# Residual picks and decoder picks turned by transposing transfers inside SBUF, decoder in blocks of four rows, a new order of steps

## The chip, the cores and the metric

The kernel runs on one core of one Trainium2 chip. The metric is the device time of one execution in microseconds (us). The text calls the engines by short names: PE is TensorE (PEld its weight loads), DVE is VectorE, ACT is ScalarE, POOL is GpSimd, SP is SyncE. SP computes nothing here; it issues transfers, in the order in which the program holds them, and SPq is that queue. A name such as L802 is line 802 of the kernel.

## The reference

A small neural codec: a depthwise convolution of three taps, SiLU, four stages of residual vector quantization with codebooks of eight entries, and a second depthwise convolution over the sum of the entries picked.

```python
B, T, D, K = 2, 16000, 512, 3
Nq, C = 4, 8

def reference(x, dw_enc, codebooks, dw_dec):
    xp = pad(x, one row of zeros before and after)
    z = silu(sum(xp[:, i:i+T, :] * dw_enc[i] for i in range(K)))
    res, q = z, 0
    for s in range(Nq):
        cb = codebooks[s]
        d2 = |res|^2 - 2 * res @ cb.T + |cb|^2        # (B, T, C), in bfloat16
        sel = cb[d2.argmin(-1)]
        q, res = q + sel, res - sel
    qp = pad(q, one row of zeros before and after)
    return sum(qp[:, i:i+T, :] * dw_dec[i] for i in range(K))
```

All tensors are bfloat16; 32,000 rows of 512 channels go in and as many come out.

## The kernel before

**Tiles.** The rows of each batch are cut into nine tiles, 18 in all; a tile holds G rows on each of 128 partitions, with G = 16 for fourteen of them and 6 and 8 for the two at each end (SIZES). GH = G/2 is the number of row pairs.

**Stages of a tile.** `load` brings x in, one transposing transfer of 128x512 for each of the G rows plus up to two for the rows at the rim (L567, L575, L581, all issued by SP), so that channels lie on partitions (XT, two buffers). `front` computes the three taps on DVE (TA, TB, L609 and L407) and the exponential on ACT (EX, L614), adds 1 (L616); `front2` takes the reciprocal on ACT (L626) and multiplies (L407): the result is Z in one of four ZB buffers. `select` runs the first three quantizer stages: products with the codebook entries and the squared norm on PE (`gram`, L638 and L645), then a chain of small DVE operations that ends in a one-hot pick (`is_equal`, L407) per stage, with a small PE transpose (L723, evicted as OT at L727 on ACT or L728 on DVE) and correction (L733) in between. `resid` forms the residual after three stages on PE: it adds Z (L796, 64x64 pieces with IDENT, UP and DOWN) and the picked rows (L802, 64x128 pieces: OHR times WR), and evicts it back into ZB (L822 on ACT, L823 on DVE). Then come the fourth stage's products and its pick (L849, L850 and L407), and `back`, the decoder: PE multiplies the picks (OHW) with a table that holds codebook entries times decoder taps (WDEC, L883, with L885 and L887 at a tile's rim), the result is evicted into YB (L892 on ACT, L893 on DVE) and stored by SP (L915; two transfers or more for four rows).

**The two turnings.** The picks come out with rows on partitions and must lie with picks on partitions to be a weight or a moving operand of PE.

- `rows`: after the third pick, OHD (the picks of three stages, each twice, 64 columns a row) is turned by GH PE transposes of 128x128 into one PSUM bank (L755) and copied into OHR by ACT or DVE (L760 where DVE does it).
- `windows`: after the fourth pick, OHA (the picks of all four stages) is turned by four PE transposes for each row pair, each filling 32 partitions (L772), and copied into OHW by ACT or DVE (L778). Each pair's window spans four rows, the pair and one neighbour on either side, so that one product of full height gives one output row: two products of 128x512 a pair, and two more at the tile's rim.

OHA is filled by DVE for stages 1, 2 and 4; POOL copies the third stage's pick from OHD into it (L715), and copies stages 1 and 2 from OHA twice into OHD (L718).

**The order.** Nothing runs in the order in which it is written. Every step is added to a `Plan` with an engine, an estimated cost, what it reads and writes and which PSUM banks it takes (four pairs of banks). `order()` then lays out one fixed sequence for each engine, by the steps' ranks (RANK) and by a model of when each can start; a step that may go to ACT or DVE (`either`: taps, plus1, OT, the copies of both turnings, evictions of resid and back) is placed by a rule of slack (SLACK) or by a list (ON_ACT, ON_DVE). SP's sequence of loads and stores is laid out in the same way. While PE would idle for long, filler products are put in (L935).

Of the kernel before, what the change touches and what calls it, by code (L numbers as in the profile page):

```python
# [16 lines left out]
class Plan:  # L17
# [10 lines left out]
    GATE = {"resid": (1.0, 2.0), "back": (1.0, 2.0), "win0": (0.6, 1.5), "win3": (0.6, 1.5), "score0": (0.25, 1.4), "score3": (0.25, 1.4)}  # L28

    def __init__(self, pairs, slack, window, quota, margin, ranks, fixed):  # L30
        self.steps, self.writer, self.readers = [], {}, {}
        self.pairs, self.slack, self.window, self.quota, self.margin, self.ranks, self.fixed = pairs, slack, window, quota, margin, ranks, fixed
# [38 lines left out]
    def order(self):  # L71
# [4 lines left out]
        assert len(rank) == len(steps)  # L76
        users = [[] for _ in steps]
# [26 lines left out]
        def look(s, e):  # L104
            t = max(at[s["n"]], clock[e])
            if s["take"]:
                if s["dest"] and held[s["dest"]] >= self.quota[s["dest"]]:
                    return inf
                t = place(s["take"][0], t)[0]
                return t + late(s["mm"], t, s["c"])  # L110
            if isinstance(s["e"], tuple) and s["n"] in self.fixed:
                if e != self.fixed[s["n"]]:
                    return inf
            elif isinstance(s["e"], tuple):
                ends = {q: max(at[s["n"]], clock[q]) + s["c"][q] for q in s["e"]}
                least, most = self.slack[s["k"][0]]
                off = ends["ACT"] - ends["DVE"]
                if (e == "ACT" and off > least) or (e == "DVE" and off <= least and off < most):
                    return inf
            if s["mm"]:  # L120
                t += late(s["mm"], t, s["c"])
            return t
# [17 lines left out]
        while len(out) < len(steps):  # L140
# [47 lines left out]
            if s["free"]:  # L188
                if s["free"]["dest"]:
                    held[s["free"]["dest"]] -= 1  # L190
                for j in s["free"]["banks"]:
                    banks[j] = end + self.LATENCY[e] + self.margin[2]
# [12 lines left out]
def kernel(  # L205
# [8 lines left out]
    nc = tc.nc  # L214
# [21 lines left out]
    SLACK = {"setup": (8.44, -17.24), "taps": (-10.16, -13.78), "plus1": (-7.56, 14.47), "decide": (9.58, -18.78), "win0": (-11.29, -2.01), "resid": (15.34, 2.59), "win3": (13.16, -12.88), "back": (17.64, 2.16)}  # L236
    QUOTA = {"ACT": 4, "DVE": 4}
    MARGIN = (0, 0, 0, 1)
    WINDOW = {"PE": 0.14, "ACT": 0.41, "DVE": 0, "POOL": 0.79, "SP": 0.05}
    DIGITS = "0123456789abcdefghijklmnopqrstuvwxyzABCDEFGHIJKLMNOPQRSTUVWXYZ"  # L240
    RANK = ("5W5X711A60616g5N69683w3x3y3z7M7N8keXeY8Y8Z909192939495969798999a9b9R9S9T9U9V9W9X9Y9Za0a1a2a3a4a5a6a7a8eZf0f1f2f3f4f5f6f7"
            "f8f9fafbfcfdfefffgfhfifjhtjikV9cflfmfnfofpfqfrfsftfufv9dfwfzfAfBfCfDfEfFfGfHfIfJfKfLfMfNfOg6g7g8g9gagbgc9egdgegfggghgigj"
            "gkglgmgngogpgqgrgsgtgugvgwgxgygzgAhZi0i1i2i3i4i5i6i7i8i9ianMnNnOnPnQnRnSnTet8CtktltmtntotptqtrknhrjUdJm7kgaLaMaN2r2s2t2v"
            "2w2x2y2z2A2B2D2E2G2H2L2M2O2P2Q2S2T2U2V2W2X2Y2Z323334353637bhbicueocvhQepluhRnzlvjyjzjAm0m1m2m37s7thShTkMkNkOnZo0o16m6d6n"
            "6l6e6k6j6h6f6iiNiOiPiQiRiSiTiUbUeFr8r9rarbrcrdrerfiitscz5Ijf9f7J7K7L3Q3R3X40444c4e4g4h4i4j4k4o4p4z4A4E4G4I4M4N4P4S4T4U4V"
            "4Z5b5g5l5o5y5z8d8ehpkxhqookyrxopsZry5q5hnEiMe41P4qdVdWbYbZdKdLdMgTgUjQjRjS6z6E6u6C6v6A6q6F6p6t6y6w6s6x6r6B6D6o7z7A7B7C7D"
            "7E7F7Gd88LdBdCdDdEdFdGdHdIjJjtks29tZ2k7eal3hdnbJrg1g1B2b4x1m1u1q0X3U1E5p0R1w3Y1peW171Uc0dw1j0O8f1VhW0U1b1avc0Q1ieV2m5rBb"
            "enhahffUejl4hbj8hhnAhLpulOpMhVn0hvlSm90ZqsqeoMsovKvSx1mvmwgBgChChDhEixiykdkekfliljmUmVmWoqorpApBpC6W6H6Z786N6O6Q6P6S6U6X"
            "6M6V6R736J6Y6T1G1J1K1IeQ3G3H2hlN3q211Z20222j3p3M26v5tyoCu1vJfW9q3ghXdb9ktj1o6I0ooR2g1v0a062n0i3s030r2o020u1H2f1O1h07050p"
            "0e0C0S0B0v0s100j0f0l5QtEcogQr3bQbeho8QbNb98vcQhwipl1jZdSpaeKeHeSkWkp8X8px4wWwUj75fidieiliminitiuiGiHiIj5j6jojpjqjKjLjWjX"  # L250
            "jYbXc1c2c3c4c5c6c7cacbcccecfchcickclcmn6nCnUn5qq1rzUwTuxvvhU11k09yBaBuBt3vij3nvCd0tHeg457n5P8I8J8K0J1d241W2c0K0Y1c19io0y"
            "1s2a1e1R2u2i1T1C0x0D0A1z4d180E0L2N3jpL1D8U7Y2C5av2s2sKs3thsLtRtiuktSuYulvruZvGvsvMvH9s8A4Yatcs8j8V7UahvbjOsPmzmAmXmYmZn3"
            "n4n9nanbndneninjnknpnqnsntnubfbgbjbkbobpbqbrbsbtbwbybAbBbCbDbEbF0N3m3k3ltg0V0T3FqNajBzujC1wcyQyBBvCct6kIk7kYpVtVaOaBw4bT"
            "bS9z4r4t53585t525K625H4W5m5YoZ7koY707PrE4s4J517o825w7f5x88878t9h5T9i8i8q7ObOmumqmTngoLpEnooT4CqZoBnWpOpHrCp2seba9B8cdveT"
            "484u311F9Gs6scfPfQhxhyhzj3j4kFkGkHmimjo6o7o8pIpJrkrlrmamanaoaqasauavayaAaCaEaGaIaKaPaRaTaUpSsDrNpZt0s0qbq2zhw5wkwKx5xewV"
            "z0yW9DA03uuV9lwJ5B7rb842dlbW4addarsx7d7h1L153d1l161n3A3L3b3E3a494R4Q5F3c2lcN3074cM2R2F1S3T3S2q25gD67o9oaobocodoeofogohoi"
            "ojokolompconnXk9jTvzr7rSqf4l5i1YeCt7t8qLqMrsrtrurGrHrVrWrXs7s8sgshsisFsGsVsWsXcAcCcDcEcFcGcIcLcOcPcRcScTcVcWcXcYcZ6a5J56"
            "5s7Vt5oXm4vq3Z5u5v8s3t9puf5Svhxq43xp5jyZ13e0e27RmSiftd76757XbLdoe38EdUcp72rOrDrRphrMkwuc7ud24H8nbM5E7c8WnYpwpxwHhd5Aib3N"
            "h0nFdsdydtdNdzdYdOecdZekedereleAeseGeB5G8z3Ib6cw8lvYwgtWrwzgzFqvqwqBqCqDqGqHqPqQqRqUqVr0r1r2r5r6rhrirj9H9I9J9K9L9M9N9O9P"
            "9Qa9aaabadaeafagn7n84b3Wu63VsE86893ewd7H5c4B5ksTte9A7l9EB377oJsdq4eDcxcyuih8h9ic4D59274X643K1k2K4y14bV2d0z3f2p9xoV5D2J3o"  # L260
            "47280M3J1X0P1N3O6b7v3i1f23bR4fmBmCmDmEmFmGmHmImJmKmLmMmNmOmPmQmR9m8x7Td3ef6cvy8B8SakvNvOqgqhrorprqrYrZslsmsnt9tatvtwtxtX"
            "tYumunuoaxazaDaFaHaJaQaSaVaWaYaZb0b1b2b3xUxVb4eyhGebeapR7isNcny0wIlJsud7dgya7jxfyhBgpzzG7WB63PdAe746kAkmyJ7Z7qw6wrhklg55"
            "5Z6L4K7y5O6KmgiknL5R8379lL4L7p7m50lPn1stnydX575V5n4OlxoEuzuAuBuC9CuDuEuFuGuHuIuJuKuLuMuNuO8y9g8acUapbIbGbvrPrBvAjaw7whwl"
            "wmwawpwnwMwBwzwXwRxgx2x9xjxixnxzxvkQkRkTkUkXkZl2l5l7l9lclelhlllnlolrlstItJp1pvC063C23ru24n7w7x841MAJcJ4mADA3qktGq9wQq8fX"
            "fSt1mrmslpsbvws1pT8T8Rbcbu9vai9FwoxmxlwCxxxNA9lEzi9obP7abHn27g8wyRzDAPbKaXcjcqvfu3u7u4uau8udubugueupuhusuquuutuwuvsssfBo"
            "qYwbltnKvgycxLyrynxGxCxExDxFxOxPxWxXxYy5y6yeyfygypyEyxzbyylTlUlWlXlYlZm5m6m8mambmcmdmemhmkmmmnyoyqy38Nq68180qpzloDwx8F85"
# [47 lines left out]
    def sb(shape, dt, name):  # L314
        return const.tile(list(shape), dt, name=name)
# [657 lines left out]
```

## Time and profile before

| | |
|---|---|
| median of 3 runs | 629.38 us (628.88 to 632.24) |
| the profiled execution | 627.0 us, its span from first to last instruction 625.1 us |
| granted TensorE clock, mean | 0.971 |
| ACT busy | 512.7 us, 82% |
| POOL busy | 79.3 us, 13% |
| transfers | 72.05 MB, 283 transposing loads, 131 stores |

How to read the views: the busy lines give microseconds, the share of the span and the number of instructions of each engine. The row of digits cuts the span into 40 equal slices of 15.6 us and gives the busy share in tenths. A group's row gives line, engine, operation, output and input with their shapes, the number of instructions, the total busy time, the mean of one in nanoseconds, and the engine's idle time just ahead of them with what ended it. The chain is followed back from the last instruction to whatever released each step. A wait view gives who waited for whom: total, times, longest.

### The profile page before, as it was taken

The numbers are of one execution on the slowest core, as the hardware profiler recorded it, in microseconds if no ns is written. First come the engines' busy times: TensorE is split into PE (matmuls) and PEld (weight loads), VectorE is DVE, ScalarE is ACT, GpSimd is POOL, SyncE is SP. The second block draws the span as 40 slices with busy tenths as digits, with TensorE's granted clock in tenths as the row PEclk, the third lists the DMA queues.
The fourth block names the chain that finished last, engine by engine and source line by source line (L and its number), as shares of the span: only waits on it lengthen the run. The fifth ranks groups of instructions, "written<-read, shape, count | busy, mean of one in ns | idle before, by whom it ended". The sixth has DMA issues, their size and how long they took to land.

```text
span 625.1 us, 26738 instructions
## 1 busy us (share of the span) xinstructions
PE 517.6 (83%) x12065; PEld 241.8 (39%) x12147; DVE 554.8 (89%) x1126; ACT 512.7 (82%) x398; POOL 79.3 (13%) x92
## 2 busy tenths in 40 slices
PE   4968867797977979788788869778979997989995
PEld 1434323433443443434334433434344344443442
DVE  6898999999989999999899999999989998984532
ACT  4454497759695999999887999998979999979765
POOL 2001000141100211101010202011022220010000
PEclk9999979898999999897799999999999999999999
DMA  5455455464461476766653585757575335042424
GB/s 115 91 98 90 101 95 86 95 176 91 78 93 44 92 184 97 193 95 185 119 142 62 82 138 94 225 96 153 94 190 88 131 62 173 3 153 94 164 98 150
DMA packets 163976, 72.05 MB, mean 115 GB/s; under 512 B 155567, under 2 KB 155599, under 8 KB 163862
## 3 DMA queue, kind: packets, MB, share of 16 engines
q1 hardware_dynamic: 163646, 69.90, 51.4%
q8 instruction: 95, 1.56, 1.1%
q10 hardware_dynamic: 216, 0.43, 0.2%
q14 instruction: 19, 0.16, 0.1%
HBM read 0.43 MB, written 32.77 MB: 53 GB/s over the span
## 4 chain that ended last, share of the span: by engine, by line
DVE 45%; PE 25%; ACT 13%; issue 7%; DMA 5%; SPq 4%; DVEq 0%; ACTq 0%
DVE ZB L407 11%; DVE TB L609 8%; PE ps L802 7%; PE ps L796 6%; PE ps L645 5%; DVE TA L407 5%; DVE TA L609 3%; ACT EX L626 3%; SPq L567 3%; DVE EX L616 3%; ACT EX L614 3%; DMA out_dram<-YB 3%; ACT YB L892 3%; PE ps L883 3%; ACT ZB L822 2%
## 5 line engine op out<-in xcount | busy, mean ns | idle before, releaser
L614 ACT ACTIVATE EX<-ZB 128x4096 bf16<-128x4096 bf16 (+2 forms) x36 | 115.1, 3199 | 35.5 <-DVE ZB L407 33.6
L802 PE MATMUL ps<-OHR,WR 64*128 64x512 bf16 (+1 forms) x1024 | 137.5, 381 | 0.9 <-issue 0.6
L892 ACT CAST YB<-ps 128x1024 bf16<-128x1024 f32 x121 | 115.5, 1027 | 17.3 <-PE ps L883 4.9
L822 ACT CAST ZB<-ps 128x1024 bf16<-128x1024 f32 (+1 forms) x121 | 116.9, 1003 | 15.1 <-PE ps L802 14.9
L626 ACT ACTIVATE EX<-EX 128x4096 bf16<-128x4096 bf16 (+2 forms) x36 | 114.7, 3195 | 0.2
L645 PE MATMUL ps<-ZB 128*32 128x64 bf16 x8064 | 90.5, 198 | 16.4 <-issue 8.8
L718 POOL COPY OHD<-OHA 128x256 bf16<-128x256 bf16 (+2 forms) x36 | 51.2, 1421 | 380.6 <-DVE OHA L407 365.3
L609 DVE TENSOR_SCALAR TB<-XT,WENC 128x2048 bf16<-128x2048 bf16 (+2 forms) x144 | 97.2, 682 | 0.2
L645 PEld LDWEIGHTS <-ZB 128*32 128x32 bf16 x8064 | 76.8, 95 | 52.0 <-issue 46.3
L935 PE MATMUL ps<-MSK,IDENT 128*128 128x512 bf16 x288 | 73.1, 393 | 11.3 <-issue 3.7
L883 PE MATMUL ps<-WDEC,OHW 128*128 128x512 bf16 x213 | 65.0, 386 | 12.1 <-ACT YB L892 3.6
L407 DVE TENSOR_TENSOR ZB<-ZB,EX 128x4096 bf16<-128x4096 bf16 (+2 forms) x36 | 72.7, 2018 | 2.0 <-ACT EX L626 1.8
L802 PEld LDWEIGHTS <-WR 64*128 64x128 bf16 x1024 | 40.1, 95 | 87.5 <-issue 61.0
L407 DVE TENSOR_TENSOR ZB<-TA,TB 128x4096 bf16<-128x4096 bf16 (+2 forms) x36 | 72.8, 2021 | 0.3
L407 DVE TENSOR_TENSOR TA<-TA,TB 128x4096 bf16<-128x4096 bf16 (+2 forms) x36 | 72.6, 2017 | 0.3
L796 PE MATMUL ps<-ZB,IDENT 64*64 64x512 bf16 (+1 forms) x512 | 51.3, 388 | 12.0 <-ACT ZB L822 5.8
L796 PE MATMUL ps<-ZB,DOWN 64*64 64x512 bf16 (+1 forms) x512 | 53.4, 404 | 0.1
L796 PE MATMUL ps<-ZB,UP 64*64 64x512 bf16 (+1 forms) x512 | 50.8, 381 | 0.0
L609 DVE TENSOR_SCALAR TA<-XT,WENC 128x2048 bf16<-128x2048 bf16 (+2 forms) x72 | 48.2, 677 | 0.6 <-DMA XT<-in_x_dram 0.3
L935 PEld LDWEIGHTS <-IDENT 128*128 128x128 bf16 x311 | 29.7, 101 | 43.2 <-issue 14.6
L616 DVE TENSOR_SCALAR EX<-EX 128x4096 bf16<-128x4096 bf16 (+2 forms) x36 | 39.4, 1095 | 3.4 <-ACT EX L614 3.4
L883 PEld LDWEIGHTS <-OHW 128*128 128x128 bf16 x252 | 21.8, 99 | 37.6 <-issue 18.4
(123 smaller groups left out, 487.5 us busy)
## 6 DMA issues: line engine op xcount, KB each, us to landing
out_dram<-YB SPq DMA_DIRECT2D x33, 448.0 KB
out_dram<-YB SPq DMA_DIRECT2D x28, 512.0 KB
XT<-in_x_dram SPq DMA_TRANSPOSE x283
out_dram<-YB SPq DMA_DIRECT2D x30, 60.0 KB
out_dram<-YB SPq DMA_DIRECT2D x31, 2.0 KB
out_dram<-YB SPq DMA_DIRECT2D x2, 224.0 KB
YB<-in_dw_dec_dram ACTq DMA_DIRECT2D x1, 384.0 KB
out_dram<-YB SPq DMA_DIRECT2D x1, 384.0 KB
```

The lines of the kernel that those rows point to most:

```text
L407: add("DVE", cost, key, lambda: nc.vector.tensor_tensor(out=out, in0=a, in1=b, op=op), reads, writes, **kw)
L609: lambda dst=dst, src=src, w=w: nc.vector.tensor_scalar(out=dst, in0=src, scalar1=w, scalar2=None, op0=ALU.mult),
L614: add("ACT", act(2 * R), ("exp", n, h), lambda: nc.scalar.activation(v(ex), Z, ACT.Exp, scale=-1.0), zt, [("EX", sl), "ACTTAB"], hold="E")
L616: lambda: nc.vector.tensor_scalar(out=ex, in0=ex, scalar1=1.0, scalar2=None, op0=ALU.add), [], [("EX", sl)])
L626: nc.scalar.add_instruction(mybir.InstActivation(name=nc.get_next_instruction_name(), engine=mybir.EngineType.Activation, func=ACT.Reciprocal,
L645: nc.tensor.matmul(o[HB * q:HB * (q + 1), u * ZW:(u + 1) * ZW].rearrange("p (s c) -> p s c", s=2), lhsT=blk, rhs=both, start=False, stop=( ...
L796: nc.tensor.matmul(ps(boxes[m])[to, 512 * u:512 * u + nk * P], lhsT=dia[h, h], rhs=Z[h, i, g0 + u:g1:2, :], start=start, stop=False)
L802: nc.tensor.matmul(ps(boxes[m])[:, 512 * u:512 * u + nk * P], lhsT=WR[v][half[u], i * P:(i + 1) * P], rhs=W[half[u], g0 // 2:g1 // 2, :], ...
L822: either({"ACT": act_psum(2 * nk * P), "DVE": dve(2 * nk * P)}, ("resid", n, m / len(units)), lambda: nc.scalar.copy(dst, src()), lambda: ...
L883: nc.tensor.matmul(o, lhsT=W[:, k, PADC:PADC + P], rhs=WDEC[u], start=True, stop=not wrap)
L892: either({"ACT": act_psum(1024), "DVE": dve(1024)}, key, lambda dst=dst, box=box: nc.scalar.copy(dst, ps(box)), lambda dst=dst, box=box: n ...
L935: nc.tensor.matmul(PS[j // 2][:, 512 * (j % 2):512 * (j % 2) + NMK * ZW], lhsT=IDENT, rhs=MSK.rearrange("p u w -> p (u w)"), start=True, s ...
```

## The change

**Turning by transfers.** `rows` issues, for each four row pairs, one transposing transfer on SP from OHD to OHR; `windows` issues one from OHA to OHW. The PE transposes, their PSUM banks and their copies on ACT or DVE are gone. A tile of 16 rows has two of the first and one of the second, each 128x512; 50 in all.

```diff
     def rows(st, key):
         n, GH = st["n"], st["GH"]
         OD, W = OHD[n % 2], OHR[n % 2]
-            for k in range(GH):
-                nc.tensor.transpose(pwb[:, k * P:(k + 1) * P], OD[:, 2 * k:2 * k + 2].rearrange("p g s c -> p (g s c)"), IDENT)
...
-        either({"ACT": act_psum(GH * P), "DVE": dve(GH * P, 1.92)}, key, lambda: nc.scalar.copy(dst, src()), lambda: nc.vector.tensor_copy(dst, src()),
-               [], [("OHR", n % 2)], free=box, after=[j])
+        for k0 in range(0, GH, 4):
+            ks = slice(k0, min(k0 + 4, GH))
+            add("SP", 1.36, key, lambda ks=ks: nc.sync.dma_start_transpose(out=W[:, ks, :],
+                in_=OD[:, 2 * ks.start:2 * ks.stop].rearrange("p g o s c -> p (g o s c)")), [("OHD", n % 2)], [("OHR", n % 2, k0 // 4)], tail=1.5)

     def windows(st, key):
-            for k in range(GH):
-                for s in range(Nq):
-                    nc.tensor.transpose(pwb[NC * s:NC * (s + 1), k * P:(k + 1) * P],
-                                        A[:, s, 2 * k:2 * k + 4, :].rearrange("p g c -> p (g c)"), IDENT)
...
+        A, W, nb = OHA[n % NOH], OHW[n % NW], (st["G"] + 3) // 4
+        add("SP", 1.36, key, lambda: nc.sync.dma_start_transpose(out=W[:, 0:nb, PADC:PADC + P], in_=A[:, 0:4 * nb].rearrange("p g s c -> p (g s c)")),
+            [("OHA", n % NOH)], [("OHW", n % NW)], tail=1.5)
```

**Layouts.** OHA becomes rows by stages by entries, without the two rim rows and their memsets; a block of four rows fills 128 columns. OHW holds GM/4 blocks instead of GM/2 windows, with 16 columns of padding on either side instead of 2. OHD's columns are two copies of four stage slots. Stages 1 and 2 write their picks into small tiles of their own (OH), and POOL's third copy brings all three stages from OHD to OHA at once.

```diff
-    OHA = [sb([P, Nq, GM + 2, C], BF16, f"OHA{b}") for b in range(NOH)]
-    PADC = 2
-    OHW = [sb([P, GHM, P + 2 * PADC], BF16, f"OHW{b}") for b in range(NW)]
+    OHA = [sb([P, GM, Nq, C], BF16, f"OHA{b}") for b in range(NOH)]
+    PADC = 16
+    OHW = [sb([P, GM // 4, P + 2 * PADC], BF16, f"OHW{b}") for b in range(NW)]
...
-    OHD = [sb([P, GM, SL, C], BF16, f"OHD{b}") for b in range(2)]
+    OHD = [sb([P, GM, 2, Nq, C], BF16, f"OHD{b}") for b in range(2)]
...
-    WDEC = [sb([P, D], BF16, f"WDEC{v}") for v in range(4)]
+    WDEC = [sb([P, D], BF16, f"WDEC{v}") for v in range(6)]
...
-                add("POOL", 1.5, key(5), lambda OH=OH: nc.gpsimd.tensor_copy(OH, OHD[b][:, 0:G, 4, :]), [("OHD", b)], [("OHA", n % NOH)])
+                add("POOL", 1.5, key(5), lambda: nc.gpsimd.tensor_copy(A[:, 0:G, 0:3, :], OHD[b][:, 0:G, 0, 0:3, :]), [("OHD", b)], [("OHA", n % NOH)])
```

**Decoder in blocks of four rows.** Windows no longer overlap. An output row has one product of full height with its own block; a row at a block's rim (its first or its last) has one more of half height (64 rows of a neighbouring block). Of a block of four rows, two full products come first, then the other two and the two halves; both pairs' evictions follow the second group. The products of all blocks are chained in order.

```diff
+        def terms(g):
+            m, r, last = g // 4, g % 4, G - 1
+            out = [(None, m, 0, r)]
+            if r == 0:
+                out.append((1, m - 1, 0, 4) if g else (last % 4 // 2, last // 4, -1, 4 if last % 4 == 3 else 5))
+            if r == 3 or g == last:
+                out.append((0, m + 1, 0, 4) if g < last else (0, 0, 1, 4))
+            return out
...
+            whole = [q for q in todo if q[3][0] is None]
+            first = whole[:2] if len(ks) > 1 else []
+            rest = whole[len(first):] + [q for q in todo if q[3][0] is not None]
+
+            def mms(group, boxes=boxes):
+                for g, i, n1, (h, blk, shift, v) in group:
+                    at = slice(None) if h is None else slice(HF * h, HF * h + HF)
+                    nc.tensor.matmul(ps(boxes[g // 2])[:, 512 * (g % 2):512 * (g % 2) + 512], lhsT=W[at, blk, PADC + shift:PADC + shift + P],
+                                     rhs=WDEC[v][at], start=i == 0, stop=i == n1)
+            j = bchain[0]
+            for k, group in zip(ks, (first, rest) if first else (rest,)):
+                j = add("PE", ...)
+            bchain[0] = j
```

**Score of the fourth stage.** Its eviction was one DVE step of two operations (L849 and L850). The second, the copy of the products into PR3, becomes a step of its own that ACT or DVE may do.

**The order.** RANK is a new string. SLACK, ON_ACT and ON_DVE are replaced by WHERE, a string with one letter for each step that may go to ACT or DVE. The windows within which the planner lets a better rank go first change a little. A PSUM bank is free once all its evictions are done.

```diff
-    WINDOW = {"PE": 0.14, "ACT": 0.41, "DVE": 0, "POOL": 0.79, "SP": 0.05}
+    WINDOW = {"PE": 0.1, "ACT": 0.43, "DVE": 0, "POOL": 0.52, "SP": 0.09}
...
-    ON_ACT = (434, 554, 564, ...)
-    ON_DVE = (374, 393, 407, ...)
+    WHERE = ("DDDDDDDDDDDDDDDDDDDDAAAAAAAADDDDDDDDDDDDDDDADADAADAAAADDDDDDDDDDDDDDDDAAAAAAAADAAAAAAAAADDDDDDDDDDDDDDDAAAAAAAAADAAAAAAAA"
...
```

234 lines of the change are left out of this document (105 added, 129 removed), and 5 rows, old and new, of the table ON_DVE.

## The prediction

> **What bounds the kernel now.** I read the busy lines first, then the table by stage, then the waits of the transfer queue SP, then the chain that ended last, and last the rows of the edited lines.
>
> ```profile
> span 625.1 us, 26738 instructions
> ...
> PE 517.6 (83%) x12065; PEld 241.8 (39%) x12147; DVE 554.8 (89%) x1126; ACT 512.7 (82%) x398; POOL 79.3 (13%) x92
> ...
> DVE  6898999999989999999899999999989998984532
> ```
>
> No engine is full over the whole span, but DVE's slices are 9 from early on until the last tenth. The next view gives busy microseconds of PE, PEld, DVE, ACT and POOL in each stretch, then the granted clock, the transfer share and GB/s.
>
> ```profile
> 100.00:513.00 413.00, 348.02 (x8725) 162.99 (x8777) 397.19 (x718) 365.60 (x253) 64.65 (x43) 0.97 0.58 119
> 513.00:550.00 37.00, 31.81 (x974) 16.43 (x980) 35.08 (x84) 34.30 (x27) 1.96 (x4) 1.00 0.24 78
> 550.00:600.00 50.00, 45.17 (x1067) 20.83 (x1073) 27.29 (x95) 39.82 (x43) 3.19 (x8) 1.00 0.37 129
> ```
>
> Two regimes. From 100 to about 550 DVE is busy 96% (397.2 of 413), and what leaves DVE there is worth its full duration, if nothing else steps in. After 550 DVE falls to 55% and PE rises to 90%. The chain confirms it: from 560 on it is PE instruction after PE instruction.
>
> ```profile
> 566.76 0.77 PE ps L796 x12
> 567.53 0.97 PE ps L802 x8
> 568.50 0.77 PE ps L796 x12
> 569.27 0.97 PE ps L802 x8
> 570.24 0.56 PE ps L772 x32
> 570.80 0.33 PE ps L755 x4
> ```
>
> The third resource is SP, whose one in-order queue issues all loads and stores. These are its longest waits between 100 and 513 (total, times, longest):
>
> ```profile
> SPq L915 <- ACT YB L892: 21.9, 7, 10.5
> SPq L567 <- DVE TB L609: 13.0, 5, 3.8
> SPq L567 <- DVE M L858: 7.0, 1, 7.0
> ```
>
> All lines of that view sum to 65 us, so SP is occupied for 413-65 = 348 us, 84%: 213 loads at 1.31 us (one issue has a median of 1.265 us, and 16 in a row take 22.6 to 22.8 where nothing disturbs them) make 279, and 77 stores take the other 69. A load in the chain lands 2.6 to 3.4 us after its issue starts. DVE does not wait for a load anywhere after 100.
>
> **Off DVE, 100 to 560.** These rows price it:
>
> ```profile
> L760 DVE COPY OHR<-ps 128x1024 bf16<-128x1024 bf16 x14 | 9.6, 685 | 4.0 <-PE ps L645 3.7 <-PE ps L755 0.2
> L850 DVE CAST PR<-ps 128x64 bf16<-128x64 f32 x30 | 6.3, 211 | 0.0
> L778 DVE COPY OHW<-ps 128x1024 bf16<-128x1024 bf16 x9 | 6.1, 680 | 1.8 <-PE ps L772 1.8
> L893 DVE CAST YB<-ps 128x1024 bf16<-128x1024 f32 x5 | 6.1, 1220 | 6.9 <-PE ps L883 6.9
> ```
>
> OHR copies: 14 x 0.68 = 9.5 us. OHW copies: 8 x 0.68 = 5.4. The PR3 copy moves to ACT in 13 of 32 cases by the string WHERE (one letter for each step that may go to either engine, read in the order in which the steps are added), 12 of them here: 12 x 0.21 = 2.5. OT copies on DVE go from 18 to 12: 1.3. One more resid eviction comes to DVE: +1.2. Back evictions on DVE go from 2 to 10: tiles 5 and 9 have one each as against two now, and tile 12 has all eight, 9.8 us. Tile 12's decoder now ends at 556.7, where DVE is already half idle, so I put those eight outside the full stage. One of the 36 additions of 1 (plus1, a small tile's) goes to ACT: 0.7. Sum: -9.5-5.4-2.5-1.3+1.2-0.7 = **-18** (with tile 12 inside, -8).
>
> ACT gives up seven OHW copies (6.3 us) and, net, nine back evictions (9 x 1.03 = 9.2); it takes six OT copies (6 x 0.27), 13 PR3 copies and one plus1 (1.9). A 128x64 PSUM copy on ACT is in no row; the 128x128 OT copy there takes 0.27, the copy on DVE 0.21, so 13 cost 2.7 to 3.5. ACT ends some 9 us lighter, and at 88% of 100 to 513 it was not the limit. I price it at 0; without the slack of DVE's and PE's work over it, it costs the 3.5.
>
> The third POOL copy grows from 128x128 (1.29 us) to 128x384: between 1.3 and 3 x 1.29 = 3.9 us. POOL idles 107 us ahead of these copies, and their reader, the turning of OHA, follows a whole residual and scoring later, so 0; uncovered it would be 2.6 a tile. Two more WDEC products (DVE 0.68 each) lie in the first 25 us, in which DVE idles 5.3: 0, uncovered +1.4.
>
> **Onto SP.** Each full tile issues two transposes of 128x512 for OHR and one for OHW. The loads are the same shape, 128x512, read from DRAM; from SBUF there is no row. I take the load's 1.31 per issue. Bounds: the store's median issue, 0.42, and one full issue for each 128x128 block, 5.2. Between 100 and 513 that adds 12 tiles' OHR (23 issues) and 11 OHW: 34 x 1.31 = 45 us, and SP's work becomes 348+45 = 393. The stage would like to shrink from 413 to 397 (18 us spread over 460). So of the 65 us that SP now waits, about 4 are left. In today's waits, 40 us are loads that wait for DVE to free their buffer; these shrink if SP is late anyway, but not to nothing. Behind a new transpose that waits for OHD stand the loads of XT, for which the taps wait, and the stores, for whose YB the evictions wait. I charge a third of the gain, **+6** (bounds 0, and all 18). The 16 transfer engines themselves have room: 0.58 of them are busy in this stage, 0.41 to 0.54 where loads run alone, so 45 us more of such issues add about 45 x 0.5 / 413 = 0.05.
>
> **The PE-bound end.** Behind 560 the chain loses L772 (0.56+0.59+0.34+0.35) and L755 (0.33+0.27): -2.4. The decoder goes from 18 full-height products on a 16-row tile to 16 full and 8 half-height. A pair of halves on different rows shares a slot if it runs as L802 does (8 in 0.97, so 0.12 each, against 0.218 for a slot, which is what one more full product adds to the chain, as L887 does at 578.95): 20 slots, +0.44 a tile, +1.3 for three tiles; the two small tiles stay equal. Full and half height alternate: resid shows that price: its unit is 8 products side by side in twos (8 x 0.109) and 12 in fours (12 x 0.0545), 1.53 us of slots, and lasts 1.74, so 0.11 for each of two switches. Two for each of 16 groups: +3.5. Sum **+2.4**; if the halves ran one after the other another 16 x 0.218 = 3.5, if switches were hidden -1.1. [...]
>
> A group of four rows now holds two PSUM pairs until its last half product. L883 waited 3.6 us for YB evictions in the whole span; doubling that bounds it at +3.6, and I take 0, since the next group only follows after two evictions anyway.
>
> **The last tile.** OHD to OHR takes 2.9 now (601.4 to 604.4) and would take about 3: 0. OHA to OHW takes 1.4 (615.0 to 616.5) and becomes 0.1 + 3.0: **+1.7**. If a store is still landing (4.15 us in the chain), up to +6; a gain is excluded, since no transfer in the chain landed in less than 2.6.
>
> **The order chosen anew** has no row. I price it at 0. From below: half of DVE's idle time before 100 (11.5 us), -6. From above: as much again, +6.
>
> **Sum.** The profiled execution took 627.0 (span 625.1 and 1.9 around it): 627.0 - 18 + 6 + 2.4 + 1.7 = 619.1. The median of the runs shown is 2.4 higher, so **621**.
>
> **Rivals.**
> 1. *SP keeps pace and the order helps.* DVE's 18 stay whole, the end costs 1.7, and 5 of the early idle time go: 627-18+1.7-5 = 605.7, as a median 608. For it: only 4 us of SP waits are needed to fit. Against it: those waits are for DVE itself.
> 2. *The queue eats the gain.* SP's 393 plus 20 of waits that stay is again 413: no gain in the stage, and the end's 4.1 is partly covered: 627+2, median 631. For it: 84% already; against it: waits for buffers shrink when the queue is late.
> 3. *In-order SP starves the taps: slower.* Place: a transpose that reaches SP before OHD or OHA is written, with the next loads behind it. PE's own turning waited for OHD 8 times, 10.8 us, 1.35 each. If half of the 34 wait so long (23 us) and 10 us of other waits stay, the stage is 393+23+10 = 426, +13, and with 4.1 at the end 644, median 646. It decides from the point where waits on SP exceed 20 us in this stage (413-393). Against it: the select of a tile lies early enough that a late issue loses nothing by itself, as four ZB buffers let taps run ahead.
> 4. *An SBUF source is issued block by block.* 34 x 4 blocks x 1.31 = 178 instead of 45: the stage becomes 348+178 = 526, +113, about 745. No row has an SBUF source; but a load's four blocks share one 1.265. [...]
>
> **Chances.** Forecast 0.42 (its own range 613 to 627, with 0.05 of it above 626), rival 1 0.19, rival 2 0.13, rival 3 0.22, rival 4 0.04. What this measurement can tell from no change is about 0.5%, 3.1 us, so faster means under 626.2: 0.37+0.19+0.02 = 0.58. Within: 0.05+0.10 = 0.15. Slower, over 632.5: 0.01+0.22+0.04 = 0.27. The range runs from 606, below which a third of rival 1 lies, to 646, above which are half of rival 3 and rival 4.
>
> **What would show it.** In the profile after: no L755 and L772 rows and no OHR or OHW copies; DVE's total near 544 (554.8, less all OHR and OHW copies 17.9, PR3 2.7, OT 1.3, plus1 0.7 and memsets 0.6, plus nine back evictions 11.0 and WDEC 1.4); DVE still 95% busy between 100 and 500. SP's new issues 1.2 to 1.4 us, its waits in the middle 20 us or less. DVE waits for XT, or taps late behind OHR transposes, show rival 3. Issues of 5 us show rival 4. PE products of the decoder of 0.12 each in pairs show the half slots right, 0.22 wrong. A DVE that idles in the middle without waiting for loads would make the forecast wrong through PE or PSUM, which I priced at 0.

## The result, and the profile after

The changed kernel is slower, by 5.4%, and outside the range that was given.

| | before | after |
|---|---|---|
| median, us | 629.76 (628.88 to 632.24, 4 runs) | 663.94 (662.18 to 666.61, 4 runs) |
| ratio to before, 95% interval | 1 | 1.054 [1.0493, 1.0586] |
| profiled span, us | 625.1 | 664.8 |
| granted TensorE clock, mean | 0.971 | 0.932 |
| last load's issue ends at, us | 513.5 | 547.0 |
| last tap starts at, us | 543.6 | 567.6 |
| from the last tap's start to the end, us | 81.5 | 97 |

The page of the profile after, span and busy times:

```profile
span 664.8 us, 25826 instructions
...
PE 537.5 (81%) x11571; PEld 234.7 (35%) x11652; DVE 552.0 (83%) x1078; ACT 504.4 (76%) x401; POOL 66.2 (10%) x93
```

DVE has lost only 2.8 us of work (554.8 before), and it is no longer full. The next view is the table by stage of the kernel after: stretch, length, busy time of PE, PEld, DVE, ACT and POOL, granted clock, transfer share, GB/s.

```profile
100.00:513.00 413.00, 323.42 (x7641) 142.94 (x7693) 375.57 (x646) 330.70 (x231) 49.87 (x38) 0.91 0.60 119
513.00:550.00 37.00, 35.25 (x741) 14.25 (x744) 30.20 (x52) 32.03 (x27) 2.55 (x4) 0.95 0.48 103
550.00:600.00 50.00, 44.30 (x1228) 20.63 (x1230) 43.48 (x110) 46.03 (x42) 4.03 (x7) 1.00 0.48 132
```

In the stage where DVE was 96% busy it is now 91% busy, and PE, ACT and POOL each do less there than before: all four are held up by something else. The full stretch runs on past 550, where DVE works 43.5 of 50 us against 27.3 before. The chain of waits says what holds them, first as shares of the span:

```profile
PE 29%; SPq 25%; DVE 22%; ACT 10%; DMA 7%; issue 6%; DVEq 0%; POOL 0%; ACTq 0%; POOLq 0%
```

Before, SPq had 4% and DVE 45%. A piece of that chain (start, duration, what), at one of the places where it runs through the queue:

```profile
370.68 1.27 SPq L560
371.99 1.27 SPq L560
373.30 1.27 SPq L560
...
378.35 1.26 SPq L560
379.65 3.46 DMA XT<-in_x_dram
...
383.43 0.76 DVE TA L602
```

The last ten loads of a tile's own rows (L560) go out one behind the other from 364.7 to 379.6, most of them every 1.3 us, with gaps of 0.35 us at the most. The load issued behind them at 379.65 (a rim row, L568) lands after 3.5 us, and the tile's first tap starts 0.3 us later. There the taps wait for the queue. The longest waits of the queue itself in 100 to 513:

```profile
SPq L904 <- ACT ZB L794: 4.0, 7, 1.8
SPq L744 <- POOL OHA L707: 3.3, 3, 1.3
SPq L560 <- DVE TB L602: 3.0, 3, 1.3
SPq L750 <- DVE OH L402: 3.0, 2, 1.8
```

All lines of that view sum to 32.9 us, against 65 before: the queue is occupied for 380 of 413 us. The new issues are as short as forecast, 1.207 us (L744, OHR, 32 of them) and 1.270 us (L750, OHW, 18) in the median.

### The profile page after: what moved, and what is told of

Its sections match the earlier page's. It is cut to its first block, busy times and chain, and to the rows that moved or that the text cites. A ratio compares the mean times of both kernels' runs of the same rounds, so it can differ in the third digit from the quotient of the medians.

```text
span 664.8 us, 25826 instructions
## 1 busy us (share of the span) xinstructions
PE 537.5 (81%) x11571; PEld 234.7 (35%) x11652; DVE 552.0 (83%) x1078; ACT 504.4 (76%) x401; POOL 66.2 (10%) x93
## 4 chain that ended last, share of the span: by engine, by line
PE 29%; SPq 25%; DVE 22%; ACT 10%; DMA 7%; issue 6%; DVEq 0%; POOL 0%; ACTq 0%; POOLq 0%
SPq L560 20%; PE ps L774 9%; PE ps L768 7%; DVE ZB L402 5%; PE ps L868 5%; PE ps L638 4%; DVE TB L602 4%; DMA out_dram<-YB 3%; ACT EX L607 2%; DVE TA L602 2%; ACT EX L619 2%; ACT ZB L794 2%; SPq L568 2%; DMA XT<-in_x_dram 2%; DMA OHR<-OHD 2%
## 5 line engine op out<-in xcount | busy, mean ns | idle before, releaser
L774 PE MATMUL ps<-OHR,WR 64*128 64x512 bf16 (+1 forms) x1024 | 142.3, 394 | 20.4 <-DMA OHR<-OHD 20.1
L881 ACT CAST YB<-ps 128x1024 bf16<-128x1024 f32 x112 | 107.9, 1021 | 38.9 <-PE ps L868 26.1
L868 PE MATMUL ps<-WDEC,OHW 128*128 128x512 bf16 (+1 forms) x339 | 91.5, 407 | 24.5 <-ACT YB L881 8.4
L924 PE MATMUL ps<-MSK,IDENT 128*128 128x512 bf16 x325 | 82.8, 397 | 16.8 <-DVE S L673 7.1
L711 POOL COPY OHD<-OH 128x256 bf16<-128x256 bf16 (+2 forms) x36 | 40.5, 1125 | 427.8 <-DVE OH L402 427.8
L402 DVE TENSOR_TENSOR TA<-TA,TB 128x4096 bf16<-128x4096 bf16 (+2 forms) x36 | 72.8, 2023 | 0.3
L868 PEld LDWEIGHTS <-OHW 128*128 128x128 bf16 (+1 forms) x380 | 26.1, 98 | 77.9 <-issue 64.2
L924 PEld LDWEIGHTS <-IDENT 128*128 128x128 bf16 x349 | 33.3, 101 | 55.6 <-issue 24.0
L821 DVE TENSOR_REDUCE rr<-ps 128x8 bf16<-128x256 f32 (+1 forms) x32 | 13.3, 415 | 38.2 <-PE ps L638 25.4
```

The source lines that it names most:

```text
L402: add("DVE", cost, key, lambda: nc.vector.tensor_tensor(out=out, in0=a, in1=b, op=op), reads, writes, **kw)
L774: nc.tensor.matmul(ps(boxes[m])[:, 512 * u:512 * u + nk * P], lhsT=WR[v][half[u], i * P:(i + 1) * P], rhs=W[half[u], g0 // 2:g1 // 2, :], ...
L868: nc.tensor.matmul(ps(boxes[g // 2])[:, 512 * (g % 2):512 * (g % 2) + 512], lhsT=W[at, blk, PADC + shift:PADC + shift + P], rhs=WDEC[v][at ...
L881: either({"ACT": act_psum(1024), "DVE": dve(1024)}, key, lambda dst=dst, box=box: nc.scalar.copy(dst, ps(box)), lambda dst=dst, box=box: n ...
L924: nc.tensor.matmul(PS[j // 2][:, 512 * (j % 2):512 * (j % 2) + NMK * ZW], lhsT=IDENT, rhs=MSK.rearrange("p u w -> p (u w)"), start=True, s ...
```

## The experiments

The ratio is to the kernel before, timed on the same chip beside it, with its 95% interval. Not all runs were on the same chip, so where two runs are compared closely, their ratios count. The wait of SP is the sum over all lines of the queue's waits between 100 and 513.

| run | median, us | ratio to before | SP waits, us | last tap, us |
|---|---|---|---|---|
| after | 663.94 | 1.054 [1.0493, 1.0586] | 32.9 | 567.6 |
| a1_no_turning | 627.39 | 0.9967 [0.9943, 0.9991] | 52.9 | 531.1 |
| a2_idle_issues | 654.34 | 1.0393 [1.033, 1.0456] | 18.8 | 553.9 |
| a3_waits_unread | 656.15 | 1.0426 [1.0384, 1.0469] | 31.2 | 557.2 |
| a4_stores_pool | 651.93 | 1.0359 [1.031, 1.0408] | 53.4 | 548.4 |
| b1_no_halves | 627.01 | 0.9985 [0.9947, 1.0024] | 67.3 | 531.7 |
| b2_before_idle | 667.71 | 1.0648 [1.0584, 1.0712] | 22.5 | 583.1 |
| b3_merged_issues | 629.58 | 1.001 [0.9977, 1.0043] | 155.6 | 530.3 |
| b4_before_merged | 625.1 | 0.9944 [0.9926, 0.9962] | 184.9 | 543.3 |
| c1_rows_only | 652.05 | 1.0372 [1.0324, 1.0421] | 33.5 | 571.6 |
| c2_rows_merged | 639.57 | 1.0169 [1.0123, 1.0216] | 186.3 | 554.1 |
| c3_idle_merged | 626.18 | 0.9957 [0.9928, 0.9986] | 142.6 | 542.1 |
| c4_evict_act | 631.75 | 1.0043 [1.0014, 1.0073] | 156.9 | 532.5 |
| d1_rows_unread | 618.4 | 0.9806 [0.9782, 0.9831] | 168.9 | 534.7 |
| d2_no_turning_merged | 627.47 | 0.997 [0.994, 0.9999] | 190.3 | 529.5 |
| d3_no_turning_light | 629.16 | 0.999 [0.997, 1.0011] | 193.2 | 533.1 |
| e1_rows_two | 633.4 | 1.0088 [1.0055, 1.0121] | 171.1 | 549.1 |
| e2_rows_act | 678.53 | 1.0813 [1.0778, 1.0848] | 197.8 | 586.7 |

In all of them the planned order of the kernel they start from is kept; only what a step emits differs.

### What the transfers cost, taken apart

**a1_no_turning.** The whole change, but the turning steps emit nothing; OHR and OHW are filled with zeros once.

```diff
-            add("SP", 1.36, key, lambda ks=ks: nc.sync.dma_start_transpose(out=W[:, ks, :], in_=OD[...]), ...)
+            add("SP", 1.36, key, lambda: None, ...)
```

> The changed kernel without any of its 50 turning transfers: OHR and OHW are filled with zeros once, so the picks take no part in residual and decoder; every other step stands where the plan puts it. Queue theory (SP is full, its issues and their waits hold up the loads and stores behind them): 620 to 632. Latency theory (a pick reaches PE later than a PE transpose brought it): also 620 to 632. Order theory (the new sequence of steps is the slower one by itself, with the transfers only as passengers): 645 or more.

**a2_idle_issues.** All 50 transfers at their places and in their sizes, from a table that is ready early into buffers that nobody reads. The picks are not turned; PE reads zeros.

```diff
-  nc.sync.dma_start_transpose(out=W[:, ks, :], in_=OD[...])
+  nc.sync.dma_start_transpose(out=scratch()[...], in_=CBX[:, 0:P * (ks.stop - ks.start)])
...
-        Z, W = zrows(st), OHR[n % 2]
+        Z, W = zrows(st), OHR[0]
```

> The 50 transfers are issued at their places, with the same shapes, but from a table that is always ready and into buffers that nobody reads; PE reads zeros, as in the run without them. Nothing waits for a pick, nothing waits for a landing: only SP's time and the transfer engines' work are left. Queue theory by occupancy: 645 to 660, most of what the transfers cost. Latency theory: 620 to 632. Queue theory by waiting (the issue that waits for its pick holds up what stands behind it): 622 to 640.

**a3_waits_unread.** The same with the real picks as source, so that SP waits for them. The turned picks are not used; PE reads zeros.

```diff
-  nc.sync.dma_start_transpose(out=W[:, ks, :], in_=OD[...])
+  nc.sync.dma_start_transpose(out=scratch()[...], in_=OD[...])
```

> The 50 transfers are issued from the real picks, so SP waits for them as before, but into buffers that nobody reads; PE reads zeros and waits for no landing. Against the run with idle issues this adds the waits on SP, against the changed kernel it takes away the landing. Waiting theory: 655 to 664. Occupancy theory: the same as with idle issues, within 5. Latency theory: 622 to 635, since nothing late is left to read.

Measured: 627.4 without transfers, 654.3 with idle issues, 656.2 with issues that wait for the picks, 663.9 with all. So of the 36.5 us that turning by transfer costs, 27 come with the bare issues, some 2 with the waits of issues for picks (the intervals of a2 and a3 overlap, so this may be nothing), and 8 with the picks arriving late for PE. The 27 hold the issues' time on the queue and the traffic of the transfers together; b2 and c3 below take these apart. And a1, which has every gain of the change and none of its transfers, gains 0.3%.

**a4_stores_pool.** The whole change with the 131 stores issued by POOL instead of SP.

```diff
-            nc.sync.dma_start(out=view[p0:p1, lo:hi, :], in_=Y[p0:p1, lo - g0:hi - g0, :])
+            nc.gpsimd.dma_start(out=view[p0:p1, lo:hi, :], in_=Y[p0:p1, lo - g0:hi - g0, :])
```

> The changed kernel whole, with its 131 stores issued by POOL instead of SP, at the same places of the sequence. This frees some 100 us of SP's time and takes the waits for evictions out of the line that the loads stand in. Queue theory: 625 to 640. [...]

651.9: 12 us of the loss come back, not all of it. POOL's busy time rises from 66 to 143 us (an issue there takes 0.59 us in the mean), and its in-order queue then waits for YB (53.6 us, 22 times) with the copies into OHA and OHD behind it. SP's queue is relieved and POOL's is held up; that this is what keeps the rest of the loss was not tested.

### Is it the queue's time?

**b2_before_idle.** The kernel before with 44 idle transposing issues of 128x512 put among the loads of all tiles but the first two, and nothing else.

```diff
             nc.sync.dma_start_transpose(out=X[:, :, g + 1, :], in_=src[g])
+            if n > 1 and g in (3, 8, 13):
+                nc.sync.dma_start_transpose(out=scratch(), in_=WR[0])
```

> The kernel before, whole, with three more transposing transfers of 128x512 issued by SP among each tile's loads (44 in all), from a table that is always ready and into buffers that nobody reads. Occupancy theory: SP has 65 us of waits between 100 and 513 and these 36 issues or so take 45 of them, so some of the slack is gone and the time rises, less than the 27 us of the changed kernel, whose sequence leaves SP less: 632 to 645. If a slot in the old sequence is free as long as the sum fits: 629 to 631.

667.7, above the range expected. 44 issues of 1.26 us are 55 us of queue time over the whole run. In the kernel before the queue waited for 65 us in the stage from 100 to 513 alone, and still 40 of the 55 us (664.9 less 625.1 in the profiled spans) appear in the total. All of the 40 lie before the last tap, which starts at 583.1 instead of 543.6.

**c3_idle_merged.** The same 44 issues, in the kernel before with two rows of x in each load. For that XT is laid out by rows instead of by channel blocks, and a load is one transpose of 128x1024:

```diff
-    XT = [sb([P, KT, GM + 2, P], BF16, f"XT{b}") for b in range(NX)]
+    XT = [sb([P, GM + 2, KT, P], BF16, f"XT{b}") for b in range(NX)]
...
-            nc.sync.dma_start_transpose(out=X[:, :, g + 1, :], in_=src[g])
+            if g % 2 == 0:
+                w = min(2, G - g)
+                nc.sync.dma_start_transpose(out=X[:, g + 1:g + 1 + w].rearrange("p g i c -> p (g i) c"),
+                                            in_=rows[:, g:g + w, :].rearrange("p g d -> p (g d)"))
```

> The kernel before with merged loads and, on top, the same 44 idle transposing issues of 128x512 at the same places as in the run that took 667.7. Bytes moved are the same as there. Theory (only the time of SP's queue counts): the issues fit into the room that merging made, 624 to 630. Rival (the transposing traffic itself slows loads or DVE): 640 or more.

626.2, no slower than before. The two kernels move the same bytes with the same idle transfers at the same places; what differs is the number of the loads' issues and, with it, the layout of XT (which costs the taps nothing that shows: in b4 below, with the same layout, TB and TA take 0.686 and 0.678 us in the mean, in the kernel before 0.682 and 0.677). In the table by stage, b2_before_idle:

```profile
100.00:513.00 413.00, 322.90 (x8037) 152.91 (x8088) 364.31 (x654) 327.65 (x226) 51.50 (x37) 0.93 0.61 123
```

and c3_idle_merged:

```profile
100.00:513.00 413.00, 343.79 (x8626) 160.82 (x8676) 396.31 (x718) 364.89 (x253) 60.94 (x43) 0.97 0.70 129
```

DVE gets 364 us of work done in the first, 396 in the second, while the transfer engines are busier in the second (0.70 against 0.61). So the cost is the time of the issues on the queue, not the traffic: the issuing time of these 44 transfers is worth some 40 us in b2_before_idle.

**b4_before_merged**, the merged loads alone, and **b3_merged_issues**, the whole change with merged loads and with OHR in one transfer a tile:

```diff
-            add("SP", 1.36, key, lambda ks=ks: nc.sync.dma_start_transpose(out=W[:, ks, :],
-                in_=OD[:, 2 * ks.start:2 * ks.stop].rearrange("p g o s c -> p (g o s c)")), ...)
+            add("SP", 1.36, key, lambda k0=k0: nc.sync.dma_start_transpose(out=W[:, 0:GH, :],
+                in_=OD[:, 0:2 * GH].rearrange("p g o s c -> p (g o s c)")) if k0 == 0 else None, ...)
```

> The kernel before with two rows of x in one load (its control: the same XT layout, whose taps read 16 pieces of 128 in place of one run of 2048). Queue theory: SP does not hold the kernel before, so 624 to 631, a little faster where loads were late. If the pieces slow the taps on DVE: 635 or more.

> The changed kernel whole, with the same bytes turned in fewer issues: two rows of x in one transfer of 128x1024 (XT laid out row by row), and OHR in one transfer instead of two; 333 issues become some 184. Queue theory, if an issue costs about the same whatever its size: SP loses some 180 us of work and the time falls to 625 to 640. If an issue's time goes with its blocks, so 2.5 us each: 655 to 668, nothing won. Latency theory: 655 to 668 in either case, or worse, since a larger transfer lands later.

b3 recovers 34 us: 629.6, 1.001 [0.9977, 1.0043]. b4 is 0.6% faster than before and beats both kernels. With this the loss is settled: it is the queue, the late picks included, since b3 still turns and reads all its picks by transfer and stands within 0.4% of the same kernel without turning (d2 below, 0.997). But b3 still does not show the gain that the change should have.

### Where the gain is

**b1_no_halves.** a1 without the half-height products of the decoder, which is left incomplete at the rims of the blocks.

```diff
                 for g, i, n1, (h, blk, shift, v) in group:
+                    if h is not None:
+                        continue
```

> The changed kernel without its turning transfers (as in the first run) and without the half-height products of the decoder, 8 on each tile of 16 rows, so that the first and last row of a block lack their neighbour's part. If those halves and the switches around them fill PE in the part after the last tap, which is where the run without transfers lost what it had gained before: 610 to 619. If the order or the doubled hold of PSUM pairs makes that part long: 625 to 629.

627.0, as a1. The half-height products do not make the end long.

**c1_rows_only.** The kernel before with the residual's picks alone turned by transfer, in its old order: the transfer is issued where the copy into OHR stood.

```diff
-            for k in range(GH):
-                nc.tensor.transpose(pwb[:, k * P:(k + 1) * P], OD[:, 2 * k:2 * k + 2]..., IDENT)
+            pass
...
+        def move():
+            for k0 in range(0, GH, 4):
+                ks = slice(k0, min(k0 + 4, GH))
+                nc.sync.dma_start_transpose(out=W[:, ks, :], in_=OD[:, 2 * ks.start:2 * ks.stop]...)
...
-        either({"ACT": ..., "DVE": ...}, key, lambda: nc.scalar.copy(dst, src()), lambda: nc.vector.tensor_copy(dst, src()),
+        either({"ACT": ..., "DVE": ...}, key, move, move,
```

> The kernel before with one part of the change alone: the picks of three stages are turned by the SBUF transfers (two of 128x512 a full tile, 32 in all), issued where the copy into OHR stood; PE transposes and the OHR copies are gone; the order of everything else, OHA, OHW and the decoder are those of before. Theory (the issues of SP's queue are the cost): 32 of the 44 issues that cost 37 us in the kernel before, so +27, less up to 9.5 of DVE copies: 640 to 655. Rival (what costs is that picks arrive late, the occupancy only mattered with idle issues at places of my choosing): 620 to 632.

652.05, inside the 640 to 655 of the queue's theory. (PE also waits 33.1 us for OHR there, so the number alone does not tell the two apart. The expectation takes the loss of b2 as 37 us; b2's medians make it 40, which moves the range by 2 us.)

**c2_rows_merged.** The same with merged loads, and OHR in one transfer of 128x1024.

```diff
-            for k0 in range(0, GH, 4):
-                ...
+            nc.sync.dma_start_transpose(out=W[:, 0:GH, :], in_=OD[:, 0:2 * GH]...)
```

> The same with two rows of x in each load (128x1024) and OHR turned by one transfer a tile (128x1024): 18 new issues, with some 140 fewer loads. Theory (with the queue relieved, work taken off a full DVE is worth its duration): 9.5 us less than the kernel before with merged loads alone (625.1): 614 to 619. Rival (the fixed order holds the gain back, another engine is as full as DVE): 622 to 630.

639.6: outside both expectations, 2.3% slower than the merged loads alone. PE's waits in c2_rows_merged:

```profile
PE ps L808 <- DMA OHR<-OHD: 27.4, 11, 4.3
```

The residual's products waited 11 times for picks to land; the copy that stood there took 0.7 us, and the landings in the chain take 2.8 to 5.0 (4.7 and 5.0 at 437 and 476). The old order puts the residual right behind the turning. The queue itself was mostly not late there: it stood waiting for OHD at 13 of the 18 issues, 91.5 us in sum.

**d1_rows_unread.** The same transfers from the same picks, but into a buffer that nobody reads. The residual reads zeros instead of the picks.

```diff
-        Z, W = zrows(st), OHR[n % 2]
+        Z, W = zrows(st), OHR[0]
...
-        OD, W = OHD[n % 2], OHR[n % 2]
+        OD, W = OHD[n % 2], OHR[1]
```

> As the run with rows turned by transfer in the old order and merged issues (639.6), but the transfers go from the real picks to a buffer that nobody reads; the residual reads a buffer filled once, so the picks subtracted are zeros. Left out: the residual's dependence on the turned picks, nothing else. Theory (that run lost by landing: PE waited 27.4 us for OHR; without it the copies taken off DVE are worth their 9.5 us against 625.1): 614 to 619. Rival (the order holds the gain back whatever DVE saves): 622 to 630. Third (waits of issues in SP's queue): 633 or more.

618.4. Against the merged loads alone the ratio to before falls from 0.9944 to 0.9806, 8.7 us of 629.8; the forecast priced the OHR copies on DVE at 9.5. The last tap starts at 534.7 instead of 543.3, and 81.1 us follow it, as in the kernel before. So work taken off the full DVE is worth about its duration, once the queue has room and nobody waits for the picks. This is not DVE's copies alone: d1 also has no PE transposes of OHD (10.4 us busy in the kernel before) and none of PE's waits for the copies (5.7 us in b4); that DVE's share decides is argued from DVE being full there, 397.6 of 413 us. Having to wait for the picks, from the issue to the landing, costs 21 us (639.6 less 618.4; 23 by the ratios).

**e1_rows_two**: c2_rows_merged with OHR in two transfers of 128x512. **e2_rows_act**: c2_rows_merged with its one transfer issued by ACT.

```diff
-            nc.sync.dma_start_transpose(out=W[:, 0:GH, :], in_=OD[:, 0:2 * GH]...)
+            for k0 in range(0, GH, 4):
+                ks = slice(k0, min(k0 + 4, GH))
+                nc.sync.dma_start_transpose(out=W[:, ks, :], in_=OD[:, 2 * ks.start:2 * ks.stop]...)
```

```diff
-            nc.sync.dma_start_transpose(out=W[:, 0:GH, :], in_=OD[:, 0:2 * GH]...)
+            nc.scalar.dma_start_transpose(out=W[:, 0:GH, :], in_=OD[:, 0:2 * GH]...)
```

> Rows turned by transfer in the old order and merged loads, as in the run of 639.6, but OHR in two transfers of 128x512 instead of one of 128x1024, so that the first half lands sooner. Theory (the landing itself, longer for the larger transfer, keeps PE): half of the 27 us of PE's waits go, 622 to 632. Rival (the transfer is late already when it is issued, behind waits of SP's queue): 636 to 643.

> The same as the run of 639.6 (one transfer of 128x1024 a tile), issued by ACT from its own place in the order instead of SP. Theory (landing): PE waits for OHR as long as before and ACT gives 18 x 1.2 = 22 us, 638 to 650. Rival (lateness on SP's queue): the waits go, 618 to 630.

e1: 633.4, five to six us better and between the two expectations; PE's waits for OHR go from 27.4 to 21.5. The size of the transfer is part of it, not half. e2: 678.5, far above both expectations. The queue's waits in e2_rows_act:

```profile
SPq L921 <- ACT YB L898: 164.8, 32, 23.9
SPq L571 <- DMA OHR<-OHD: 99.7, 11, 25.3
```

The second line is new: the loads on SP wait until ACT's transposes have landed, 99.7 us in 11 places, up to 25.3 us at a time. Much of the longest of these waits must pass before ACT comes to its issue at all: a transfer of this size landed within 2.8 to 5.0 us in c2. So here a second queue did not relieve the first. What happens without these waits was not tried.

**c4_evict_act.** b3 with four of tile 12's eight decoder evictions emitted on ACT instead of DVE.

```diff
-  lambda dst=dst, box=box: nc.vector.tensor_copy(dst, ps(box))
+  lambda dst=dst, box=box, k=k: nc.scalar.copy(dst, ps(box)) if n == 12 and k % 2 else nc.vector.tensor_copy(dst, ps(box))
```

> The whole change with merged issues (629.6), with four of the eight decoder evictions of tile 12 that the new plan gave to DVE emitted on ACT, at the same places of the order. Theory (the new plan gave DVE's freed time back to evictions, and DVE sets the time there): 4 x 1.22 off DVE, 623 to 627. Rival (at that stage ACT and PE are as full as DVE, so the evictions only change the engine that waits): 628 to 635.

631.75, no gain against b3: these evictions are not what holds that kernel.

**d2_no_turning_merged** is a1 with merged loads, **d3_no_turning_light** the same without half-height products, both with edits shown above.

> The whole change without the 50 turning transfers (627.4) and with two rows of x in each load. Left out: the turning; OHR and OHW hold zeros. Theory (in the new order PE, not DVE or the queue, ends the run): 624 to 629. Rival (the loads' queue still held that kernel back): 612 to 621.

> The same without the decoder's half-height products, 26 us of PE busy time less. Left out: the turning and those products. Theory (PE's load sets what follows the last tap): 612 to 620. Rival (the fixed order with its chains of small steps sets it, as in the run without halves and with single loads, 627.0): 622 to 627.

627.5 and 629.2. Neither the queue nor late picks keep the new order from its gain, and leaving out the half products does not bring it: d3 misses the 612 to 620 of its theory. The table by stage of d2_no_turning_merged, behind its last tap at 529.5:

```profile
530.00:570.00 40.00, 37.95 (x934) 16.84 (x934) 31.89 (x92) 35.73 (x35) 3.23 (x8) 1.00 0.36 128
570.00:600.00 30.00, 30.00 (x541) 11.57 (x544) 5.78 (x26) 19.78 (x23) 0.77 (x3) 1.00 0.23 81
600.00:628.00 28.00, 18.95 (x344) 7.42 (x333) 7.38 (x16) 14.36 (x17) 0.00 (x0) 0.89 0.48 157
```

PE is busy 86.9 us after 530, all of 570 to 600 among them, and from 570 on DVE nearly idles (13 of 58 us). In the kernel before PE is busy 80.9 us in the same three stretches, in d1_rows_unread 72.8. So in the new order DVE is through its taps 14 us sooner, but PE is not further along at 530 than it was. Counted from the last tap, PE still has 67.8 us of work in the kernel before and 69.2 in d1, and 81 to 82 us pass to the end; in a1 and d2 it has 87.1, and some 97 us pass. This fits an end that waits for PE: what DVE saved was spent on running ahead with the taps. It is read from the traces and not shown. In d3, without the half products, PE has 82.3 us left behind the last tap, which itself comes 3.6 us later than in d2, and the run is no shorter. Why the new order leaves PE more to do behind the taps stays open; which of its ranks do it was not tried.

## Why the prediction was wrong

**What bounds the kernel** was read rightly for DVE, and too narrowly for the queue. DVE was the limit of 100 to 550: in d1 9.5 us taken off it go with 8.7 us less in all.

**The step that failed is "+6" for SP.** It set the issues' time against the sum of the queue's waits: 348 us occupied, 45 more, "so of the 65 us that SP now waits, about 4 are left". Each of the pieces was right (issues of 1.2 to 1.27 us, 348 occupied), and the conclusion was not, because the waits are not slack that can be spent anywhere. A tile's loads can begin only when DVE frees XT, they then go out behind one another, and the taps wait for them, so an issue that lies inside such a run makes the taps late. b2 shows the size of it without any other part of the change: of 55 us of issues 40 reach the total. a2 less a1 gives 27 for the change's own 50 issues, some 61 us of queue time. Where the forecast put 6, turning by transfer costs 36.5 (the change less a1). The sum of waits does not tell either way: after, a2, a3, b2 and c1, with 19 to 34 us of them left, lose 3.7 to 6.5%, but a4 loses 3.6% with 53.4 where a1 with 52.9 loses nothing, and c2 loses 1.7% with 186. No run got the sum below 18.8 us, however late its queue was. The sentence that 40 of these 65 us were waits for DVE's buffers, which "shrink if SP is late anyway", was the right observation and spoke for a late queue being paid for by DVE, not against it.

**Off DVE, -18.** The copies left as forecast (OHR and OHW together 17.9), and the decoder's evictions brought 10.6 against 11.0. DVE's total still fell by 2.8 instead of the 10.8 that the forecast of 544 stood for; the rest are rows that no term had: MV, UP, SEL and DOWN, the same instructions at the start, take 5.5 longer, and TB, TA and E about 2.5 in sum. In the change as it stands nothing of the 18 can show; without its transfers (a1) the last tap comes 12.5 us sooner, which is what can be seen of it at the taps; the new order has a share in these 12.5 that was not separated. Nothing speaks against putting tile 12's evictions outside the full stage: moving four of them to ACT gains nothing (c4).

**The order chosen anew, 0,** was the second error: with the queue relieved and no transfers left in, the new order ends at 627.5 (d2). Its part after the last tap is 96.5 us in a1 against 81.5 before, +15, which eats the 12.5. The bounds of -6 and +6 did not hold it. What makes that part long stays open (d3).

**The PE-bound end, +2.4.** The transposes left it, and PE's total still rose, from 517.6 to 537.5: the decoder's products take 96.1 us busy on L868 (69.6 at full height, 26.5 at half) against 76.3 before on L883, L885 and L887, the turnings 21 less, the filler products 9.7 more. The prices of the term were right: in the trace after, a pair of halves at 570.12 takes 0.39 us together, as long as one product alone, so it shares a slot, and the product before it starts 0.31 us earlier and the one behind it 0.32 us later, against 0.22 between full ones, which is 0.10 for each switch. But leaving the halves out (b1, d3) changes the time by nothing that can be measured, so the term's size mattered to no number here.

**The landing, +1.7** for the last tile, was priced at one place only. The 8 us between a3 and the change are late picks at all tiles: PE waits 20.1 us for OHR in 5 places, the longest 6.8. In the old order it would have been more (21 us in c2).

**The rivals.** Rival 3, slower through an in-order queue that starves the taps, named the place, and with 646 a price nearer to the result than any other. Its mechanism is only half confirmed: the issue that waits for its pick with loads behind it costs some 2 us (a3 less a2); the loads are late because of the issues' bare time. Its point of decision, 20 us of waits on SP, is passed with 32.9. Rival 2 had the right cause, the queue, and stopped at no gain. Rival 1 and the forecast are excluded. Rival 4 is excluded by the issues' 1.21 us: no price had to be paid for each block of 128x128, since an issue of two, three or four blocks took about the same 1.2 us (1.18 to 1.30 for two, 1.18 and 1.19 for three, and 1.21 and 1.27 in the median of all OHR and all OHW issues, most of them of four). What decided was the queue on which it stood, and the landing.

**Of the signs named in advance,** the L755 and L772 rows are gone, the issues take 1.2 to 1.27, DVE is 91% busy instead of 95, and its total is 552 instead of 544. The sign for rival 3 shows weakly in the waits, since DVE's direct waits for XT are only 2.3 us; it is the chain that shows it, with SPq's share at 25%.

## What to carry to other kernels

The summed waits of an in-order queue are not room for more issues (here 65 us of them, and of 55 us of added issues 40 reached the total, b2): look where in a tile the issues fall, and whether a full engine waits for the last of a run. Where a queue is 84% occupied with issues, as here, make fewer and larger ones first (two rows a load and one OHR transfer a tile made the change 34 us faster), and only then give it new work. Before replacing a copy of 0.7 us by a transfer, see how soon its reader follows: in an order made for the copy, the landing of 3 to 5 us is paid on the path, and in an order made for the transfer, look what else that order gives up.

## What the runs showed of the hardware

- The issue of a transposing transfer hardly depended on its size here: in the median 1.2 to 1.27 us for 128x256 to 128x512 from SBUF or DRAM (after: OHR 1.207, OHW 1.270, loads 1.265), and 1.24 for 128x1024 from SBUF (c2). Loads of 128x1024 from DRAM took 1.24 to 1.31 one alone (three in c2; two others 1.77 and 2.05), and mostly 1.4 to 1.8 each in a run of six or eight (b4, c2).
- A transposing transfer from SBUF to SBUF landed about as late as a load: 2.3 to 4.5 us after its issue started for 128x512 in c1, 2.4 to 4.0 in the kernel after, 2.8 to 5.0 for 128x1024 in c2, against 2.6 to 3.4 for loads in the kernel before and 3.5 to 4.2 in the kernel after (where the chain passes through them).
- In 100 to 513 the granted clock was 0.91 and 0.93 where PE is busy 323 us (after, b2), 0.94 and 0.95 at 334 and 340 us (a2, c2), and 0.97 at 344 to 352 (before, c3, a1, d1); in a4 it was 0.94 at 348. What this adds to the loss was not separated.
